# Fused attention and two feed-forward layers on one core: who adds the small constant to the row sums, and when the reciprocals stand in VectorE's queue

## The chip, the core and the metric

The kernel runs on one core of a Trainium2 chip. A core has TensorE (PE, matrix products into PSUM; its weight loads are listed as PEld), VectorE (DVE), ScalarE (ACT), GpSimd (POOL) and SyncE (SP, which issues most DMA transfers). Each engine works through its own queue in order; semaphores tie the queues together. The metric is the time of one execution in microseconds.

## The reference

Inputs are `q`, `k`, `v` (2 x 8 x 768 x 64), 16 cluster centroids per head, and the weights of two feed-forward layers. All is fp32.

```
q_assign, k_assign = argmax over the 16 normalised centroids, per head and token
scores = where(q_assign == k_assign, q @ k.T / 8, -1e9)
attn   = exp(scores - rowmax)
attn   = attn / (sum(attn) + 1e-9)          # the constant that is moved
x      = (attn @ v), heads side by side     # 1536 x 512
x      = rational(x @ w_in) @ w_out         # first layer, 512 -> 2048 -> 512
out    = layernorm(h * softmax(h)) @ w2_out # second layer, h = x @ w2_in, 512 -> 1024 -> 512
```

## The kernel before

Attention runs as 96 units: 16 heads (head `n` is batch `n // 8`, head `n % 8`) of 6 units (`t` = 0 to 5), each of 128 query rows by 768 keys. Unit number `idx` is 6n + t. For a unit TensorE computes the scores, negated and masked, in two halves of 384 columns (`unit_scores`, L405 and L411); VectorE takes the row minimum of that (`unit_max`, L416; called the unit's maximum below); ScalarE takes the exponent into `p` and adds up each row into a column of `rs` (`unit_exp`, L426). Every two units VectorE transposes `p` in 32 x 32 blocks into `pt` (`turn_p`, L454), and TensorE multiplies that with `v` a head later (`pv_step`, L466). The scores live in two PSUM slots `s` that take turns, so the scores of a unit wait for the exponent of the unit two before.

`rs[key]` holds the row sums of the two heads 2 key and 2 key + 1. They are whole after the last unit of the odd head, and are used in the next even head, 2 key + 2, whose units are 12 key + 12 to 12 key + 17. In its unit 0 `pair_sums` (L490) has GpSimd add the constant 1e-9 (L494) and puts the reciprocal on VectorE behind the maximum of its unit 2 (`step(12 * key + 14, "dve", ...)`, L495). `sums_out` (L505) puts the rest two steps on: in front of the scores of unit 3 TensorE turns the 128 x 12 reciprocals (`turned`, L511), into the free columns of that unit's PSUM slot; behind unit 3's exponent ScalarE copies them out (`rt`, L516), and SyncE sends them to DRAM (`rd`, L518) and back, spread over 64 partitions each (`rb`, L521). GpSimd then scales the pair's output with it (`pair_fin`, L539 and L553). For the last pair (key 7) ScalarE adds the constant (L497) and no DRAM is used.

GpSimd also prepares the operands of each head one head ahead (`prep_head`: L358 three times, L372, L377). With it go the mask rows, which SyncE copies into the prepared tiles (L381, L382). Between these stand parts of the weight conversion of the first layer (L149, L152, L164 on ScalarE, L156 on VectorE, L157 and L165 on GpSimd).

The order of each engine's queue is set when the program is built, by a scheduler that follows the order of the code and these constraints: `step(u, e, f)` issues `f` in unit `u` right behind that unit's instruction on engine `e`; `tc.issue_after(x)` holds what is issued inside it behind `x`; `behind` does so for one instruction. Without such a bound the scheduler may place an instruction earlier or later in its queue.

Of the kernel before, what the change touches and what calls it, by code (L numbers as in the profile page):

```python
# [10 lines left out]
AF = mybir.ActivationFunctionType  # L11
ALU = mybir.AluOpType
# [18 lines left out]
def fused_kernel(ctx: ExitStack, tc: tile.TileContext, qT, kT, v, cent, w1, w2i, w2o, gln, coef, centT, cst, tri, out):  # L31
    nc = tc.nc
# [14 lines left out]
    def psum2(tag, name):  # L47
        return ps[tag].tile([128, 2, 512], F32, name=name, tag=tag, bufs=2)
# [38 lines left out]
    tiny = const.tile([128, 1], F32, name="tiny")  # L87
# [105 lines left out]
    last = {}  # L193

    def load_pairs(es, parts=1):
        for pp, i in es:
            b, p = divmod(pp, 4)
            t = asp.tile([128, S], F32, name=f"pr{pp}{i}", tag="pr", bufs=4)
            raw["p", pp, i] = t
        w = S // parts  # L200
        for c in range(parts):
            for pp, i in es:
                b, p = divmod(pp, 4)
                nc.sync.dma_start(
                    out=raw["p", pp, i][:, w * c:w * c + w],
                    in_=(qT, kT)[i][b, 2 * p:2 * p + 2].rearrange("j d t -> (j d) t")[:, w * c:w * c + w])

    def load_head(n):
        b, h = divmod(n, H)
        for i, src in enumerate((qT, kT)):  # L210
            t = qk.tile([128, S], F32, name=f"dup{n}{i}", tag=f"dup{i}", bufs=2)
            if n:
                nc.sync.dma_start(out=t[0:64], in_=src[b, h])
            nc.sync.dma_start(out=t[64:128], in_=src[b, h])
            raw["d", n, i] = t

    def load_v(n):

        b, h = divmod(n, H)
        t = vp.tile([128, S // 32, D], F32, name=f"v{n}", tag="v", bufs=2)  # L220
        for r in range(4):
            nc.sync.dma_start(out=t[32 * r:32 * r + 32], in_=v[b, h])
        vv[n] = t
# [68 lines left out]
    def by_token(k, t, o):  # L292
        M = 32 * len(sets[k])
        return nc.tensor.transpose(o, E[k][0:M, t * 128:(t + 1) * 128], ident[0:M, 0:M])
# [69 lines left out]
    def prep_head(n, er=None, es=None):  # L364
        er = er or nc.gpsimd
        es = es or nc.gpsimd
        b, h = divmod(n, H)
        i = n % NB
        a, c = raw.pop(("d", n, 0)), raw.pop(("d", n, 1))
        rnd(er, k1[i], c, sgn[:, 1:2])  # L370
        yield
        es.tensor_tensor(k2[i][0:64], c[0:64], k1[i][0:64].bitcast(F32), op=ALU.subtract)  # L372
        yield
        rnd(er, q1[i], a, sgn[:, 0:1])
        rnd(er, q2[i][0:64], a[0:64], -0.125)
        yield
        es.tensor_tensor(q1[i][64:128], a[64:128], q1[i][64:128].bitcast(F32), op=ALU.subtract)  # L377
        yield
        if n:
            assert masked[next(k for k, es in enumerate(sets) if (n // 2, 0) in es)] == S  # L380
            nc.sync.dma_start(out=k2[i][64:80].bitcast(F32), in_=mk.pop((n, 1)).bitcast(F32))  # L381
            last["mk"] = last["mk", n] = nc.sync.dma_start(out=q2[i][64:80].bitcast(F32), in_=mk.pop((n, 0)).bitcast(F32))  # L382
        yield
# [13 lines left out]
    def unit_scores(n, t):  # L397
        i = n % NB
        sp = psum2("s", f"s{n}_{t}")
        sl = slice(t * 128, (t + 1) * 128)  # L400
        before = None
        for f in pre.pop(n * NT + t, ()):
            before = f(sp) or before
        for a in range(2):
            r = nc.tensor.matmul(sp[:, a, 0:384], lhsT=q1[i][:, sl], rhs=k1[i][:, a * 384:(a + 1) * 384], start=True, stop=False)  # L405
            if a == 0:
                last["pe0"] = r
            if before:
                behind(r, before)
        for a in range(2):  # L410
            last["pe"] = nc.tensor.matmul(sp[:, a, 0:384], lhsT=q2[i][:, sl], rhs=k2[i][:, a * 384:(a + 1) * 384], start=False, stop=True)  # L411
        return sp
# [20 lines left out]
    def step(u, e, f):  # L433
        steps.setdefault((u, e), []).append(f)
# [55 lines left out]
    def pair_sums(key):  # L490

        r = rs.pop(key)
        if key < 7:
            nc.gpsimd.tensor_scalar(r, r, 1.0, 1e-9, op0=ALU.mult, op1=ALU.add)  # L494
            step(12 * key + 14, "dve", lambda: nc.vector.reciprocal(r, r))  # L495
            return r
        nc.scalar.activation(out=r, in_=r, func=AF.Identity, bias=tiny)  # L497
        nc.vector.reciprocal(r, r)

        rw = fin.tile([128, S], F32, name="rw", tag="rb", bufs=1)  # L500
        nc.vector.tensor_copy(rw.rearrange("p (t j d) -> p j t d", t=NT, j=2), r[:, :, :, None].to_broadcast([128, 2, NT, D]))
        rb = psum2("s", "rbp")
        rsd[key] = rb, rw

    def sums_out(key, r, u):  # L505

        w = []

        def turned(sp):
            w.append(sp)  # L510
            return nc.tensor.transpose(sp[0:12, 0, 384:512], r.rearrange("p j t -> p (j t)"), ident)  # L511

        def spread_out():
            sp = w[0]
            rt = sm.tile([12, 128], F32, name=f"rt{key}", tag="rt", bufs=2)
            nc.scalar.activation(out=rt, in_=sp[0:12, 0, 384:512], func=AF.Copy)  # L516
            d = dram.tile([2, S], F32, name=f"rd{key}", tag="rd")
            nc.sync.dma_start(out=d.rearrange("j (t p) -> (j t) p", p=128), in_=rt)  # L518
            rb = fin.tile([128, S], F32, name=f"rb{key}", tag="rb", bufs=1)
            for j in range(2):  # L520
                nc.sync.dma_start(out=rb[64 * j:64 * j + 64], in_=d[j:j + 1, :].to_broadcast([64, S]))  # L521
            rsd[key] = rb

        while u in pre:
            u += 1
        pre[u] = [turned]
        step(u, "act", spread_out)
# [32 lines left out]
    def spread(gen, n, i0, i1, plan=plan):  # L560
        for i in range(n):
            plan[min(96, i0 + (i1 - i0) * i // n)].append(gen)
# [70 lines left out]
    for a in range(2):  # L633
        tps.append(bank(f"a{a}", f"set0{a}")[:, 0:3 * M].rearrange("p (t m) -> p t m", t=3))
        for t in range(3):
            r = by_token(0, 3 * a + t, tps[a][:, t])
# [98 lines left out]
    for idx, (n, t) in enumerate(units):  # L735
        if idx == ACL:
            asg.close()
            wh["r"] = ctx.enter_context(tc.tile_pool(name="wh2", bufs=4, side="right"))
        if idx in PAIRS:
            with tc.issue_after(last["mk"].ins):  # L740
                load_pairs(sets[PAIRS[idx]])
        if t == 3 and 0 < n < B * H - 2:
            with tc.issue_after(last["mk", n].ins):
                load_head(n + 2)
        if t == 0:
            if n >= 1 and n + 1 < B * H:
                spread(prep_head(n + 1), 7, idx, idx + 6)
        if t == (4 if n + 1 < B * H else 3):
            with tc.issue_after(last["mk"].ins):
                load_v(n)  # L750
        sp = unit_scores(n, t)
        run_steps(idx, "pe")
        m = unit_max(n, t, sp)
        run_steps(idx, "dve")
        if n == B * H - 1 and t >= NT - 2:
            if t == NT - 2:
                for _ in turn_p(n, NT // 2 - 2):
                    pass
            else:
                end = turn_p(n, NT // 2 - 1)  # L760
                next(end)
        elif t % 2 and idx > 1:
            for _ in turn_p(*divmod(idx // 2 - 1, NT // 2)):
                pass
        if idx == 8:
            with tc.issue_after(last["act"].ins):
                nc.scalar.activation(out=ab, in_=coef_t[:, 4:6], func=AF.Abs)

        m_, i0, i1 = pv_part(n, t)
        if m_ >= 0:  # L770
            for i in range(i0, i1):
                pv_step(m_, i)
        unit_exp(n, t, sp, m)
        run_steps(idx, "act")
        if t == 0 and n and n % 2 == 0:
            sums_out(n // 2 - 1, pair_sums(n // 2 - 1), idx + 3)
        for i, f in zip(SET1, (set1_a, set1_b, set1_c)):
            if idx == i:
                f()
        if n >= 2 and t == 1:  # L780
            for i in range(2):
                with tc.issue_after(last["act"].ins):
                    pv_out(n - 2, i)
            if n % 2:

                fin_ = pair_fin(n // 2 - 1)
                for i in (2, 3, 4, 5):
                    plan[min(96, idx + i)].append(fin_)
        run_plan(idx)
        if idx == 1:  # L790
            set1_0()
            with tc.issue_after(last["act"].ins):
                nc.scalar.activation(out=trib, in_=tri_t, func=AF.Copy)
# [369 lines left out]
```

## Time and profile before

| | us |
|---|---|
| runs shown | 648.45, 650.13, 650.15 (median 650.13) |
| the profiled execution | 653.5 |
| its span, first to last instruction | 651.6 |
| TensorE busy in it | 606.2 (93%) |
| VectorE busy | 478.6 (73%) |
| ScalarE busy | 443.3 (68%) |
| GpSimd busy | 393.6 (60%) |

The mean granted clock of TensorE is 0.982 of full speed. Busy times say which engine has much to do, not what a given stretch waits for; for that the rows below are read. In a row of a timeline the first number is the start in us from the first instruction of the span, the second the duration; the engine, the line of the kernel, the operation and its output and inputs follow, with the count of merged instructions, and in brackets how long the engine had been idle and which instruction ended that. A busy share of TensorE counts matrix products whose ends are modelled.

### The profile page before, as it was taken

The numbers are of one execution on the slowest core, as the hardware profiler recorded it, in microseconds if no ns is written. First come the engines' busy times: TensorE is split into PE (matmuls) and PEld (weight loads), VectorE is DVE, ScalarE is ACT, GpSimd is POOL, SyncE is SP. The second block draws the span as 40 slices with busy tenths as digits, with TensorE's granted clock in tenths as the row PEclk, the third lists the DMA queues.
The fourth block names the chain that finished last, engine by engine and source line by source line (L and its number), as shares of the span: only waits on it lengthen the run. The fifth ranks groups of instructions, "written<-read, shape, count | busy, mean of one in ns | idle before, by whom it ended". The sixth has DMA issues, their size and how long they took to land.

```text
span 651.6 us, 13967 instructions
## 1 busy us (share of the span) xinstructions
PE 606.2 (93%) x5601; PEld 480.0 (74%) x5601; DVE 478.6 (73%) x633; ACT 443.3 (68%) x804; POOL 393.6 (60%) x345
## 2 busy tenths in 40 slices
PE   7788888788976899999999999999999999999998
PEld 6466666566654688788888888886888888888887
DVE  3688789778968779887979878779798645344350
ACT  3567578657858678989988879789796334444251
POOL 5955588848979557998889988777976000000000
PEclk9799999989979899999999999999999999999999
DMA  8967968776765241221213323223000000000001
GB/s 207 226 169 189 246 160 238 188 183 174 203 160 122 74 165 65 98 96 66 97 65 99 97 65 97 65 65 89 10 1 1 1 18 16 33 17 17 32 16 49
DMA packets 22584, 64.79 MB, mean 99 GB/s; under 512 B 4548, under 2 KB 5784, under 8 KB 22520
## 3 DMA queue, kind: packets, MB, share of 16 engines
q1 hardware_dynamic: 22088, 63.73, 35.4%
q8 instruction: 44, 0.72, 0.5%
q10 hardware_dynamic: 432, 0.17, 0.1%
q14 instruction: 20, 0.16, 0.1%
HBM read 59.23 MB, written 3.19 MB: 96 GB/s over the span
## 4 chain that ended last, share of the span: by engine, by line
PE 54%; DVE 4%; ACT 4%; POOL 3%; issue 1%; POOLq 0%; DVEq 0%; ACTq 0%
PE y L912 16%; PE h L805 14%; PE hh L1000 10%; PE o L1051 10%; PE lt L1033 2%; PE pv L466 1%; POOL gl L895 1%; POOL q L876 1%; DVE q L887 1%; ACT y L874 1%; DVE vw L160 1%; DVE xhl L718 1%; POOL q L875 1%; ACT t L873 1%; DVE h L888 1%
## 5 line engine op out<-in xcount | busy, mean ns | idle before, releaser
L426 ACT ACTIVATE p<-s,m 128x768 f32<-128x768 f32 x96 | 86.1, 899 | 69.5 <-DVE m L416 69.1
L416 DVE TENSOR_REDUCE m<-s 128x1 f32<-128x768 f32 x96 | 88.9, 944 | 29.0 <-PE s L411 29.0
L805 PE MATMUL h<-xhl,w1h 128*128 128x512 f32 x336 | 106.5, 393 | 0.1
L466 PE MATMUL pv<-pt,v 32*64 32x192 f32 x3072 | 84.6, 339 | 4.8 <-ACT w L484 3.6
L454 DVE STREAM_TRANSPOSE pt<-p 128x1536 f32<-128x1536 f32 (+1 forms) x49 | 84.9, 1733 | 0.2 <-ACT p L426 0.2
L895 POOL TENSOR_TENSOR gl<-y,gh 128x512 fp32r<-128x512 f32 x48 | 71.3, 1488 | 16.7 <-ACT gh L894 16.5
L466 PEld LDWEIGHTS pv<-pt,v 32*64 32x64 f32 x3072 | 60.0, 134 | 23.2 <-issue 14.6
L805 PEld LDWEIGHTS h<-xhl,w1h 128*128 128x128 f32 x336 | 62.8, 188 | 14.9 <-DVE y L889 0.5
L405 PE MATMUL s<-k,q 128*128 128x384 f32 x192 | 59.6, 393 | 11.0 <-ACT p L426 10.1
L912 PE MATMUL y<-gl,w1h 128*128 128x512 f32 x168 | 66.1, 393 | 1.3 <-POOL gl L895 1.3
L876 POOL TENSOR_TENSOR q<-q,t 128x512 f32<-128x512 f32 x48 | 64.4, 1342 | 2.9
L912 PE MATMUL y<-gh,w1l 128*128 128x512 f32 x168 | 65.8, 392 | 0.0
L805 PE MATMUL h<-xhl,w1l 128*128 128x512 f32 x168 | 65.6, 392 | 0.0
L912 PE MATMUL y<-gh,w1h 128*128 128x512 f32 x168 | 61.7, 392 | 0.0
L875 POOL TENSOR_SCALAR q<-t,ab 128x512 f32<-128x512 f32 x48 | 42.3, 880 | 21.9 <-ACT t L873 16.2
L405 PEld LDWEIGHTS s<-k,q 128*128 128x128 f32 x192 | 31.0, 197 | 32.1 <-ACT p L426 18.0
L411 PE MATMUL s<-k,q 128*128 128x384 f32 x192 | 51.4, 351 | 1.7 <-POOL k L631 1.7
L1000 PE MATMUL hh<-vh,xhl 128*128 128x512 f32 x160 | 51.0, 395 | 0.0
L877 DVE TENSOR_TENSOR y<-y,h 128x512 f32<-128x512 f32 x48 | 32.8, 684 | 24.3 <-ACT y L874 24.0
L887 DVE SCALAR_TENSOR_TENSOR q<-q,h 128x512 f32<-128x512 f32 x47 | 32.0, 682 | 11.5 <-ACT h L885 11.0
L912 PEld LDWEIGHTS y<-gl,w1h 128*128 128x128 f32 x168 | 31.5, 188 | 9.6 <-POOL gl L895 2.7
L411 PEld LDWEIGHTS s<-k,q 128*128 128x128 f32 x192 | 36.5, 197 | 2.0 <-POOL k L631 2.0
(190 smaller groups left out, 1408.4 us busy)
## 6 DMA issues: line engine op xcount, KB each, us to landing
raww<-in_w SPq DMA_DIRECT2D x32, 512.0 KB, 3.7
v<-in_v SPq DMA_DIRECT2D x64, 192.0 KB, 5.9
dup<-in_qT SPq DMA_DIRECT2D x31, 192.0 KB, 5.8
dup<-in_kT SPq DMA_DIRECT2D x31, 192.0 KB, 5.1
rawv<-in_w2i SPq DMA_DIRECT2D x8, 512.0 KB, 3.6
rawv<-in_w2o SPq DMA_DIRECT2D x8, 512.0 KB, 3.6
out<-ob SPq DMA_DIRECT2D x11, 256.0 KB, 2.0
pr<-in_qT SPq DMA_DIRECT2D x7, 384.0 KB, 5.4
```

Source lines behind the costliest of these rows:

```text
L405: r = nc.tensor.matmul(sp[:, a, 0:384], lhsT=q1[i][:, sl], rhs=k1[i][:, a * 384:(a + 1) * 384], start=True, stop=False)
L411: last["pe"] = nc.tensor.matmul(sp[:, a, 0:384], lhsT=q2[i][:, sl], rhs=k2[i][:, a * 384:(a + 1) * 384], start=False, stop=True)
L416: last["dve"] = nc.vector.tensor_reduce(m, sp[:, :, 0:384], axis=AX.XY, op=ALU.min)
L426: last["act"] = nc.scalar.activation(out=P[n, t // 2][:, t % 2], in_=sp[:, :, 0:384], func=AF.Exp, scale=-1.0, bias=m, accum_out=rs[key][: ...
L454: r = nc.vector.transpose(PT[n][:, 2 * i + m * a:2 * i + m * a + m].rearrange("p t k -> p (t k)"), p[:, m * a:m * a + m].rearrange("p t a ...
L466: last["pv"] = nc.tensor.matmul(pv[n][64 * c:64 * c + 64, r, 0:192].rearrange("p (t q) -> p t q", t=NT), lhsT=vv[n][sl, j], rhs=PT[n][sl, ...
L805: r = nc.tensor.matmul(hp, lhsT=w[:, kt * 128:(kt + 1) * 128], rhs=x[:, kt], start=(i == 0), stop=(i == 11))
L876: nc.gpsimd.tensor_tensor(q, q, t, op=ALU.mult)
L895: nc.gpsimd.tensor_tensor(gl, y, gh.bitcast(F32), op=ALU.subtract)
L912: nc.tensor.matmul(o, lhsT=w[:, c], rhs=g, start=(first and i == 0), stop=(last and i == 2))
L1000: last["th"] = nc.tensor.matmul(hp[:, a], lhsT=y[:, kt], rhs=w[:, 512 * a:512 * a + 512], start=(kt == 0 and e == 0), stop=(kt == 3 and e ...
L1051: r = nc.tensor.matmul(op[:, 0:m], lhsT=l[:, kt], rhs=w, start=(n == 0), stop=(n == 23))
```

## The change

The constant is added by ScalarE for all pairs, by one ACTIVATE with function Identity and the constant as bias, issued behind the exponent of unit 0 of the even head. The reciprocal of pairs 0 to 6 is put behind the maximum of unit 1 of that head, where it stood behind that of unit 2. The transpose on TensorE stays in front of unit 3.

```diff
     def pair_sums(key):
 
         r = rs.pop(key)
+        nc.scalar.activation(out=r, in_=r, func=AF.Identity, bias=tiny)
         if key < 7:
-            nc.gpsimd.tensor_scalar(r, r, 1.0, 1e-9, op0=ALU.mult, op1=ALU.add)
-            step(12 * key + 14, "dve", lambda: nc.vector.reciprocal(r, r))
+            step(12 * key + 13, "dve", lambda: nc.vector.reciprocal(r, r))
             return r
-        nc.scalar.activation(out=r, in_=r, func=AF.Identity, bias=tiny)
         nc.vector.reciprocal(r, r)
...
         if t == 0 and n and n % 2 == 0:
-            sums_out(n // 2 - 1, pair_sums(n // 2 - 1), idx + 3)
+            with tc.issue_after(last["act"].ins):
+                sums_out(n // 2 - 1, pair_sums(n // 2 - 1), idx + 3)
```

The order that comes of it is shown for head 14 (pair 6). On VectorE, `m14_0` to `m14_3` are the maxima of units 0 to 3, `pt13` the transposed exponents of head 13, `rs6` the row sums of heads 12 and 13, and `w1f4` a weight in conversion. Before:

```order
L416 TENSOR_REDUCE m14_0_2971<-s14_0_2966 128x1
L416 TENSOR_REDUCE m14_1_2984<-s14_1_2979 128x1
L454 STREAM_TRANSPOSE pt13_2862<-p13_4_2919 128x1536
L416 TENSOR_REDUCE m14_2_3031<-s14_2_3026 128x1
L495 RECIPROCAL rs6_2589<-rs6_2589 128x12
L156 TENSOR_SCALAR w1f4_286<-w1f4_286 128x512
L416 TENSOR_REDUCE m14_3_3045<-s14_3_3039 128x1
```

VectorE at the same place now:

```order
L416 TENSOR_REDUCE m14_0_2971<-s14_0_2966 128x1
L416 TENSOR_REDUCE m14_1_2984<-s14_1_2979 128x1
L454 STREAM_TRANSPOSE pt13_2862<-p13_4_2919 128x1536
L495 RECIPROCAL rs6_2589<-rs6_2589 128x12
L416 TENSOR_REDUCE m14_2_3032<-s14_2_3027 128x1
L156 TENSOR_SCALAR w1f4_286<-w1f4_286 128x512
L416 TENSOR_REDUCE m14_3_3045<-s14_3_3039 128x1
```

The reciprocal has moved ahead of the maximum of unit 2, and stands behind the transpose. In heads 4 to 12 it is the same; in head 2 it stands ahead of the transpose as well.

On GpSimd, in the same head, `k11`, `q11`, `q21` and `k21` are the operands of head 15. Before:

```order
L358 TENSOR_SCALAR q21_170<-dup150_2849 64x768
L372 TENSOR_TENSOR k21_172<-dup151_2852,k11_171 64x768
L377 TENSOR_TENSOR q11_169<-dup150_2849,q11_169 64x768
L494 TENSOR_SCALAR rs6_2589<-rs6_2589 128x12
L157 TENSOR_TENSOR w1f4_286<-w1f4_286,raww141_2847 128x512
```

The addition stood behind the whole preparation of head 15 and is gone from this queue; the rest is in the old order. On ScalarE it appears behind the exponent of unit 0 of head 14 (`p14_0`, which the exponents of units 0 and 1 share; `u6` and `w6` are the product with `v` of head 12 being copied out):

```order
L426 ACTIVATE p14_0_2974,rs7_2973<-s14_0_2966,m14_0_2971 128x768
L493 ACTIVATE rs6_2589<-rs6_2589,tiny_94 128x12
L426 ACTIVATE p14_0_2974,rs7_2973<-s14_1_2979,m14_1_2984 128x768
L484 ACTIVATE u6_3021<-pv12_2864 64x4x6x32
L484 ACTIVATE w6_3022<-pv12_2864 64x4x6x32
```

Nothing else has moved on ScalarE, and SyncE's queue is as it was.

## Rows read from the trace of the kernel before

**Rows 1.** Summary of waits: engine, line, releaser; total us, times, longest us.

```profile
DVE m L416 <- PE s L411: 29.0, 40, 2.4
PE s L511 <- DVE rs L495: 18.4, 7, 4.9
DVE rs L495 <- POOL rs L494: 8.0, 3, 3.2
```

**Rows 2.** Table by stretch: heads 4, 8, 10, 12, 13, 14, first scores to first scores.

```profile
core 0: us, PE busy (x) PEld busy (x) DVE busy (x) ACT busy (x) POOL busy (x), PEclk, DMA share, GB/s
69.19:82.53 13.34, 11.58 (x254) 8.43 (x250) 10.27 (x11) 8.01 (x18) 6.46 (x7) 1.00 0.95 207
120.89:138.10 17.21, 13.79 (x254) 10.07 (x250) 10.64 (x12) 9.20 (x20) 10.50 (x10) 0.80 0.96 229
152.72:164.33 11.61, 9.96 (x225) 7.48 (x217) 10.74 (x12) 9.11 (x19) 8.51 (x8) 1.00 0.66 159
175.87:192.64 16.77, 11.94 (x226) 8.81 (x218) 10.98 (x12) 9.74 (x20) 13.07 (x13) 0.80 0.79 192
192.64:204.13 11.49, 10.04 (x225) 7.47 (x217) 11.34 (x11) 9.63 (x19) 10.82 (x10) 1.00 0.49 120
204.13:220.55 16.42, 11.49 (x226) 8.55 (x218) 10.98 (x12) 9.75 (x20) 12.28 (x11) 0.90 0.26 69
```

**Rows 3.** Timeline of TensorE, units 3 and 4 of heads 6, 8, 12, 14.

```profile
102.97 0.59 PE L405 MATMUL s<-k,q 128*128 128x384 f32 x2
...
105.00 0.62 PE L405 MATMUL s<-k,q 128*128 128x384 f32 x2
...
129.01 0.37 PE L511 MATMUL s<-cst,rs 128*12 128x128 f32 x1 [3.11 <-DVE rs L495]
...
184.83 0.37 PE L511 MATMUL s<-cst,rs 128*12 128x128 f32 x1 [4.75 <-DVE rs L495]
...
213.21 0.37 PE L511 MATMUL s<-cst,rs 128*12 128x128 f32 x1 [4.86 <-DVE rs L495]
213.23 0.99 PE L405 MATMUL s<-k,q 128*128 128x384 f32 x2
...
216.75 0.62 PE L405 MATMUL s<-k,q 128*128 128x384 f32 x2
```

**Rows 4.** Timeline of GpSimd in head 14.

```profile
210.71 1.80 POOL L377 TENSOR_TENSOR q<-dup,q 64x768 fp32r<-64x768 f32 x1
212.60 0.20 POOL L494 TENSOR_SCALAR rs<-rs 128x12 f32<-128x12 f32 x1
```

**Rows 5.** Timeline of VectorE in heads 6 and 14.

```profile
101.75 0.92 DVE L416 TENSOR_REDUCE m<-s 128x1 f32<-128x768 f32 x1
102.59 0.21 DVE L495 RECIPROCAL rs<-rs 128x12 f32<-128x12 f32 x1
...
103.95 0.96 DVE L416 TENSOR_REDUCE m<-s 128x1 f32<-128x768 f32 x1 [0.86 <-PE s L411]
...
207.02 1.76 DVE L454 STREAM_TRANSPOSE pt<-p 128x1536 f32<-128x1536 f32 x1
...
212.83 0.23 DVE L495 RECIPROCAL rs<-rs 128x12 f32<-128x12 f32 x1 [3.21 <-POOL rs L494]
...
214.90 0.96 DVE L416 TENSOR_REDUCE m<-s 128x1 f32<-128x768 f32 x1 [1.56 <-PE s L411]
```

**Rows 6.** Timeline of ScalarE: unit 0 of head 14; the addition for the last pair.

```profile
206.32 0.90 ACT L426 ACTIVATE p<-s,m 128x768 f32<-128x768 f32 x1 [0.36 <-DVE m L416]
207.12 0.19 ACT L426 ACTIVATION_READ_ACCUMULATOR p<-s,m 128x1 f32 x1
...
233.37 0.31 ACT L497 ACTIVATE rs<-rs,tiny 128x12 f32<-128x12 f32 x1
233.58 0.79 ACT L484 ACTIVATE u<-pv 64x768 f32<-64x768 f32 x1
```

**Rows 7.** Timeline of SyncE's queue in head 13 (spread sums, mask rows of head 14).

```profile
193.22 1.10 SPq L521 DMA_DIRECT2D rb<-rd  x2
...
195.01 0.58 SPq L382 DMA_DIRECT2D q<-oh  x1
```

**Rows 8.** DMA issues by line: count, KB each, median us from issue to landing.

```profile
q<-oh SPq DMA_DIRECT2D x15, 48.0 KB, 4.2
```

## The prediction

> **What bounds the kernel now.** I read the summary of waits first [rows 1], then the heads one by one in a table by stretch [rows 2], then each engine's timeline around the seven places where a reciprocal of row sums is taken. The program is 16 heads of attention, one after the other, and then the two feed-forward layers; the change touches heads alone, so the question is what a head is waiting for.
>
> The reader is to see in [rows 1] that TensorE stood still 18.4 us over exactly 7 occurrences, each time before the small transpose of the reciprocals (L511), and each time until VectorE had taken the reciprocal (L495). In three of the seven VectorE itself waited for GpSimd's addition (L494), 8.0 us together. [rows 3] has three of TensorE's seven waits: 3.11 us in head 8, 4.75 in head 12, 4.86 in head 14. The other four, in heads 2, 4, 6 and 10, share 18.4 - 12.72 = 5.7 us, 1.4 each.
>
> What makes GpSimd late is shown for head 14 in [rows 4]: the addition is a 0.20 us instruction that starts at 212.60, directly behind the last step of preparing head 15 (210.71 + 1.80 = 212.51). It waits for nothing but its place in the queue; the row sums of heads 12 and 13 were complete before head 14's first exponent at 206.32 [rows 6]. VectorE stops at its reciprocal from 209.6 to 212.83 [rows 5], and since TensorE's transpose stands ahead of the scores of unit 3, the maximum of unit 3 comes at 214.90. [rows 2] has the price in whole heads: 16.77 and 16.42 us for heads 12 and 14 against 11.61 for head 10, which has the same instructions but a GpSimd that was in time, and 17.21 for head 8 against 13.34 for head 4, its like (both also carry the similarities of a later set).
>
> The price is more than the idle time. In [rows 2] the granted clock of heads 8, 12 and 14 is 0.80, 0.80 and 0.90, so part of each ran at the lower level of 1.2 GHz; heads 4, 10 and 13, in which TensorE had no such gap, have 1.00, which is 2.4 GHz. [rows 3] shows it in the work: from the scores of unit 3 to those of unit 4 head 6 needs 105.00 - 102.97 = 2.03 us, head 14 behind its gap 216.75 - 213.23 = 3.52, so 1.49 more.
> The Trainium skill (TensorE: Matmul & The Clock Gate, HAM oscillation) says that the array's clock falls to half after TensorE has stood idle and that the work after the gap starts cold; the trace agrees, with 3.52 us against 2.03. By that page the slow stretch would go with the gap; without it only the idle 12.7 us would.
>
> **The change part by part.** *GpSimd's addition goes.* Seven instructions of 0.20 us, 1.4 us of queue; by itself worth nothing, since GpSimd is not what ends a head (0 to 1.4).
>
> *ScalarE gets it, behind the first exponent of the even head.* The one case in the trace is the addition for the last pair, L497: 0.31 us, the next instruction 0.21 us after it [rows 6]. So seven times 0.21 of queue and 0.31 until the result. In head 14 the exponent of unit 0 starts at 206.32; with its 0.90, the 0.19 of reading out the sum and 0.31 the addition would be done at about 207.7. The exponent of unit 1 moves back by 0.21 (1.5 us over seven heads, if nothing covered it). The cover is VectorE's transpose of 1.76 us from 207.02 to 208.78 [rows 5]: the reciprocal now stands behind it and ahead of the maximum of unit 2, so it finds its operand ready with 1.06 us to spare. In head 2 the order puts it ahead of the transpose; there I allow 0.2, the length of the reciprocal. If the cover were gone, each place would lose what ScalarE is late.
>
> *VectorE's reciprocals come one unit sooner.* Same number, same 0.23 us. In front of unit 2's maximum it delays that by 0.2, and no longer delays the transposed sums.
>
> *The three late places.* Head 14 step by step: the reciprocal can start at 208.78; from its start to TensorE's transpose it takes 213.21 - 212.83 = 0.38 [rows 3, 5], so TensorE goes on at 209.16 rather than 213.21: 4.05 us. With the slow 1.49 us that is 5.5. By whole heads it is 16.42 - 11.61 = 4.81 plus what head 10 itself gains (0.8, next part): 5.6. The two agree, and I take the heads: 5.6 for head 14; 16.77 - 11.61 + 0.8 = 5.96 for head 12; 17.21 - 13.34 + 0.8 = 4.7 for head 8. Sum 16.2. From below this is bounded by GpSimd's 8.0 us alone, from above by the idle 12.7 + 3 x 1.49 = 17.2.
>
> *The four other places.* Head 6 shows them [rows 5]: the maximum of unit 2 starts at 101.75 and holds the reciprocal up by its 0.84 us (next start 102.59); after it VectorE waits 0.86 us for the scores of unit 3. With the reciprocal ahead of that maximum the scores come about 0.8 earlier and VectorE can use it. 4 x 0.8 = 3.2, between 0 and the 5.7 of TensorE's waits.
>
> *What is late next.* Together 19.4 us, from which I take three things. VectorE is busy 10.98 us in heads 12 and 14 [rows 2], and the forecast lengths, 16.77 - 5.96 and 16.42 - 5.6, are both 10.8: 0.3 off for the two. The mask rows of the next head come through SyncE's queue behind the row sums' way through DRAM [rows 7]: at the start of head 13 SyncE issues the spread of the sums at 193.22 and the last mask rows of head 14 at 195.01, landing 4.2 us later [rows 8] at 199.2. Head 14 starts at 204.13 today; 5.96 earlier is 198.2. That chain begins with the exponent of unit 3, which moves too, but SyncE has loads in front that do not: 0.5 off. And in heads 4 and 8 the DMA engines are already busy 0.95 and 0.96 of the time [rows 2]; head 8's 16.5 us of transfers do not fit into 12.5, so loads have to move into neighbours (head 10 has 0.66): 0.6 off. That leaves **18.0 us**.
>
> The profiled execution took 653.5 us (span 651.6): 653.5 - 18.0 = 635.5. It was 3.4 us above the median of the three runs, 650.13; the saving belongs to both alike, so I forecast 650.1 - 18.0 = **632.1 us**. The saving passes to the end because everything behind the heads is released by their last unit.
>
> **The rivals.**
> *Given back to the next limit.* GpSimd is busy 13.07 + 10.82 us in heads 12 and 13 [rows 2], 23.9 us, and the forecast wants these two heads in 28.3 - 6.0 = 22.3. It prepares head 15 by 212.5, 8.0 us ahead of need (220.55), and the two savings take 11.6 from that need, so GpSimd must come 3.5 us earlier by closing its idle 3.7 + 0.7: it fits with 0.9 to spare. If it does not, heads 12 and 13 end at 23.9, a saving of 4.4. If also the transfers of head 8 stay where they are, it saves 17.2 - 16.5 = 0.7 and heads 2, 4 and 6 nothing. 0.7 + 4.4 + 5.6 + 0.8 = 11.5 us, 638.6; with less of each, 8 to 15, that is 635 to 642. For it: the thin margins. Against: head 13 and head 10 already run at 11.5 us with the same loads per head.
> *More than forecast.* Nothing is late next and the four short waits go whole: 17.2 + 5.7 = 22.9, 627.2. Against: VectorE is busy 10.74 of head 10's 11.61, so a head has less than a microsecond left to lose.
> *No change.* The reciprocal's wait would have to be hidden already, or its place taken by one just as long. Against: heads of equal work differ by 5 us just where GpSimd is late. 650.
> *Slower.* The reciprocal now waits for ScalarE with the maximum of unit 2, its exponent and the next scores queued behind it. With a margin of 1.06 us, a ScalarE that reaches the addition d us later than in the trace costs 7 x (d - 1.06); this eats the 18.0 from d = 3.6 on, and at d = 5 the kernel takes 650.1 + 27.6 - 18.0 = 659.7. For it: the addition's 0.21 us and the weight conversions stand in the same queue. Against: ahead of the exponent of unit 0 ScalarE waits 0.36 us for VectorE [rows 6], so it is not late at all.
> The same page of the Trainium skill (A second HAM failure mode) warns that many short idles can also make the clock swing; no head with waits of 1.4 us shows that here (1.00 in heads 4 and 10).
>
> **How the numbers follow.** Forecast 0.68, with 15 to 20.5 us saved, 629.6 to 635.1. Given back 0.18, more 0.07, no change 0.04, slower 0.03. The range that leaves out some two in ten takes in half of the giving back and of the excess: 628.5 to 639.5. About 0.3%, 2 us, is what can be told from no change here: faster 0.93, same 0.04, slower 0.03.
>
> **What would show it.** Right: no wait of VectorE's reciprocals for any engine, TensorE's waits before the transpose under 6 us in all; heads 12 and 14 between 10.8 and 11.6 us, head 8 between 12 and 13, the granted clock 1.00 in all three; the first feed-forward product of TensorE some 18 us earlier. Wrong in part: TensorE waiting for the next head's prepared operands or mask rows at the start of heads 9, 13, 14 or 15, or heads 8 and 12 stretched with the DMA share near 1. Wrong altogether: reciprocals waiting for ScalarE, or heads shorter and the feed-forward layers longer by the same amount.

## The result, and the profile after

The changed kernel takes 641.72 us, median of six runs (639.90 to 643.57), against 650.14 of the kernel before beside it. The ratio is 0.9858, with a 95% interval of 0.9811 to 0.9906: 1.4% faster, where 2.8% was forecast (632.1 us). The time lies above the range given. The profiled execution took 641.27 us with a span of 639.5; against the 651.6 of before that is 12.1 us, but the profiled execution of before lay 3.4 us above its median, so 8 to 9 us is the size to explain against 18.0. Where in the program those 3.4 us lie no run shows. In the two profiles 1.0 of the 12.1 us lies ahead of the first scores of head 1 (29.20 and 28.20), where nothing was changed and the order of the queues is the same; the other 11.1 lie in heads 1 to 15, and what follows the first product of the feed-forward layers (232.59 and 220.47) takes 419.0 us in both.

The summary of waits of the changed kernel answers to [rows 1] (the reciprocal is now L495, TensorE's transpose L510, the product with `v` still L466):

```profile
PEld pv L466 <- DMA v<-in_v: 4.7, 8, 1.0
...
PE s L510 <- DVE rs L495: 2.5, 4, 0.7
...
PE pv L466 <- DMA v<-in_v: 2.3, 6, 0.7
```

What the change says it does has happened. No reciprocal waits for another engine any more, and TensorE's waits ahead of the small transpose fell from 18.4 us to 2.5. New are the two rows with `v<-in_v`: TensorE waits for the load of `v`, 4.7 us in its weight loads and 2.3 us in its products. These overlap, so they are not to be added. The summary of before has no such row at all.

The table by heads (columns as in [rows 2]; heads 4, 8, 10, 12 and 14) tells where:

```profile
66.99:80.48 13.49, 12.46 (x254) 8.82 (x250) 10.14 (x11) 8.05 (x19) 6.43 (x6) 1.00 1.01 214
117.96:133.65 15.69, 14.08 (x253) 9.66 (x249) 11.48 (x12) 9.41 (x21) 11.88 (x11) 0.89 0.90 215
148.31:159.09 10.78, 10.04 (x226) 7.49 (x218) 10.77 (x12) 9.34 (x20) 8.35 (x8) 1.00 0.76 179
170.56:186.16 15.60, 14.29 (x225) 9.88 (x218) 12.13 (x12) 9.94 (x21) 14.53 (x14) 0.78 0.80 205
196.91:208.38 11.47, 10.23 (x226) 7.54 (x218) 11.47 (x12) 9.71 (x21) 11.16 (x10) 1.00 0.33 79
```

Head 14 went from 16.42 to 11.47 us with the granted clock at 1.00. Head 8 went only from 17.21 to 15.69 and head 12 from 16.77 to 15.60; both still have stretches at the lower clock (mean 0.89 and 0.78: with two levels, 1.00 and 0.50, that is 3.5 and 6.9 us at the lower one). Head 4 did not get shorter (13.34 to 13.49), with the DMA engines busy all the time.

TensorE's timeline in heads 8, 12 and 14 of the changed kernel, beside [rows 3]:

```profile
122.80 0.27 PE L510 MATMUL s<-cst,rs 128*12 128x128 f32 x1
...
123.27 0.51 PE L411 MATMUL s<-k,q 128*128 128x384 f32 x2
124.18 0.51 PE L466 MATMUL pv<-pt,v 32*64 32x192 f32 x2 [0.41 <-DMA v<-in_v]
124.86 0.53 PE L466 MATMUL pv<-pt,v 32*64 32x192 f32 x2 [0.17 <-DMA v<-in_v]
126.06 2.78 PE L466 MATMUL pv<-pt,v 32*64 32x192 f32 x44 [0.67 <-DMA v<-in_v]
126.64 1.59 PEld L466 LDWEIGHTS pv<-pt,v 32*64 32x64 f32 x42 [0.39 <-DMA v<-in_v]
...
176.41 1.18 PE L466 MATMUL pv<-pt,v 32*64 32x192 f32 x4
178.00 2.72 PE L466 MATMUL pv<-pt,v 32*64 32x192 f32 x44 [0.42 <-DMA v<-in_v]
...
201.82 0.27 PE L510 MATMUL s<-cst,rs 128*12 128x128 f32 x1 [0.41 <-DVE rs L495]
...
203.03 1.24 PE L466 MATMUL pv<-pt,v 32*64 32x192 f32 x48 [0.23 <-ACT w L484]
```

In head 14 the transpose, the scores of unit 3 and the 48 pieces of the product run on without a stop for `v`. In heads 8 and 12 the product of that same unit starts, stops for one of the four loads of `v` after the other (the last stop shows in the weight loads, PEld, alone), and its last 44 pieces then take 2.78 and 2.72 us where 48 take 1.24 in head 14: the idle time, and the lower clock behind it, have moved from the transpose to the product right behind it.

Why `v` comes then is in SyncE's queue. In the kernel before, the loads of the `v` of heads 7 and 11, which heads 8 and 12 multiply in unit 3, stand there so:

```profile
121.39 1.76 SPq L222 DMA_DIRECT2D v<-in_v  x4
...
173.77 1.76 SPq L222 DMA_DIRECT2D v<-in_v  x4
```

For those of head 7 the view of DMA issues gives the median time to landing (last number, us):

```profile
v<-in_v SPq DMA_DIRECT2D x4, 192.0 KB, 8.0
```

And TensorE's timeline has the two products that use them:

```profile
130.60 2.58 PE L466 MATMUL pv<-pt,v 32*64 32x192 f32 x48
...
186.41 2.22 PE L466 MATMUL pv<-pt,v 32*64 32x192 f32 x48
```

SyncE's queue at the same place of the changed kernel, and the `v` of head 11:

```profile
107.66 0.30 SPq L517 DMA_DIRECT2D rd<-rt  x1
111.82 1.10 SPq L520 DMA_DIRECT2D rb<-rd  x2
...
114.28 0.54 SPq L213 DMA_DIRECT2D dup<-in_kT  x1
...
117.15 0.54 SPq L132 DMA_DIRECT2D raww<-in_w  x1
117.79 1.76 SPq L222 DMA_DIRECT2D v<-in_v  x4
...
169.96 1.76 SPq L222 DMA_DIRECT2D v<-in_v  x4
```

The median time to landing for head 7 there:

```profile
v<-in_v SPq DMA_DIRECT2D x4, 192.0 KB, 7.4
```

In head 8 `v` was in time before only because the late transpose had pushed the product back: the last of the four loads landed at 130.9, the product started at 130.60, 9.7 us into the head. Now the product could start at about 124, 6 us into the head, and the last load lands only at 126.6, at the last stop in the rows above. In head 12 there was room before: `v` was whole at 182.1, 4.3 us ahead of the product. That room is gone from both sides. The product comes 4.7 us sooner within the head (5.8 us behind its first scores, 10.5 before), and `v`, issued 3.8 us sooner for a head that starts 5.3 us sooner, is whole 1.7 us later within it (7.9 us in, 6.2 before): the heads have become shorter, SyncE's queue has not kept up. Ahead of the loads of head 7 in the queue stand the row sums' way through DRAM (the spread of the sums, behind the write of 107.66, is not issued before 111.82), then 4 x 192 KB of `q` and `k` for head 10 and 512 KB of weights. The chain of waits over heads 4 to 14 goes through the `v` of heads 3, 7 and 11 (7.68, 7.34 and 7.11 us) and through that way through DRAM (4.14).

### The profile page after: what moved, and what is told of

The parts are those of the page before. It is cut to its first block, busy times and chain, and to the rows that moved or that the text cites. A ratio compares the mean times of both kernels' runs of the same rounds, so it can differ in the third digit from the quotient of the medians.

```text
span 639.5 us, 13958 instructions
## 1 busy us (share of the span) xinstructions
PE 607.1 (95%) x5601; PEld 478.6 (75%) x5601; DVE 480.1 (75%) x633; ACT 444.3 (69%) x811; POOL 392.6 (61%) x338
## 4 chain that ended last, share of the span: by engine, by line
PE 62%; DVE 14%; ACT 8%; DMA 6%; POOL 4%; issue 4%; SPq 2%; ACTq 0%; POOLq 0%; DVEq 0%
PE y L912 16%; PE h L805 15%; PE hh L1000 10%; PE o L1051 10%; DVE m L416 5%; DVE pt L454 4%; PE pv L466 4%; DMA v<-in_v 3%; ACT p L426 3%; PE s L405 2%; PE lt L1033 2%; PE s L411 2%; POOL gl L895 1%; DMA pr<-in_kT 1%; POOL q L876 1%
## 5 line engine op out<-in xcount | busy, mean ns | idle before, releaser
L466 PE MATMUL pv<-pt,v 32*64 32x192 f32 x3072 | 88.3, 337 | 7.5 <-ACT w L484 4.7
L466 PEld LDWEIGHTS pv<-pt,v 32*64 32x64 f32 x3072 | 61.1, 133 | 28.6 <-issue 13.4
L895 POOL TENSOR_TENSOR gl<-y,gh 128x512 fp32r<-128x512 f32 x48 | 71.3, 1489 | 16.7 <-ACT gh L894 16.5
L405 PE MATMUL s<-k,q 128*128 128x384 f32 x192 | 58.4, 386 | 11.3 <-ACT p L426 10.6
L405 PEld LDWEIGHTS s<-k,q 128*128 128x128 f32 x192 | 29.7, 191 | 33.1 <-ACT p L426 18.8
L411 PE MATMUL s<-k,q 128*128 128x384 f32 x192 | 49.9, 342 | 2.0 <-POOL k L630 2.0
L894 ACT ACTIVATE gh<-y 128x512 fp32r<-128x512 f32 x48 | 29.8, 628 | 11.6 <-DVE y L889 11.5
```

Of the source, the lines that this page charges most:

```text
L466: last["pv"] = nc.tensor.matmul(pv[n][64 * c:64 * c + 64, r, 0:192].rearrange("p (t q) -> p t q", t=NT), lhsT=vv[n][sl, j], rhs=PT[n][sl, ...
L895: nc.gpsimd.tensor_tensor(gl, y, gh.bitcast(F32), op=ALU.subtract)
```

## The experiments

Ratios are to the kernel before, timed beside each run; its median was 650.1 to 653.3 us, so runs are compared by ratio. The line numbers are those of the changed kernel unless said otherwise.

**The two halves apart.** ScalarE's addition alone, with the reciprocal left behind the maximum of unit 2:

```diff
-            step(12 * key + 13, "dve", lambda: nc.vector.reciprocal(r, r))
+            step(12 * key + 14, "dve", lambda: nc.vector.reciprocal(r, r))
```

> The changed kernel with the reciprocals back behind the maximum of unit 2: only the engine of the addition is changed against before. Theory (what mattered is GpSimd's queue): the reciprocals no longer wait for another engine, the three long idles of TensorE go, heads 2, 6 and 10 keep their short one of about 1.4 us; 642 to 646. Rival (the place of the reciprocal is what gave the time): above 647.

Measured: 644.30 us, ratio 0.9866 (0.9820 to 0.9911), not to be told from the whole change. Its waits, and heads 8 and 12:

```profile
PE s L510 <- DVE rs L495: 9.5, 7, 1.6
```

```profile
124.43:137.13 12.70, 11.11 (x253) 8.24 (x249) 10.90 (x12) 9.41 (x21) 9.36 (x9) 1.00 0.85 206
176.36:187.98 11.62, 9.98 (x226) 7.49 (x218) 11.53 (x12) 9.83 (x21) 11.47 (x10) 1.00 0.52 124
```

So the same time comes about in another way. The two heads are short, at full clock, and no wait of TensorE for `v` is listed in the whole run: the product comes about 1 us later within the head than in the changed kernel, and `v` is whole 6.3 and 5.1 us into it, where it takes 8.6 and 7.9 there. The time is lost in heads 1, 4, 6 and 10 instead (14.48, 15.25, 13.15 and 13.24 us, against 12.91, 13.34, 11.61 and 11.61 before). In head 6 the clock falls behind a wait of 1.56 us for the reciprocal (mean 0.87); in heads 4 and 10 TensorE also stands 1.33 and 1.39 us in a product for nothing that the profile shows. Why these stops and the loss in head 1 came in that execution stays open.

And the kernel before with only the reciprocal one unit sooner, behind GpSimd's addition:

```diff
-            step(12 * key + 14, "dve", lambda: nc.vector.reciprocal(r, r))
+            step(12 * key + 13, "dve", lambda: nc.vector.reciprocal(r, r))
```

> The kernel before with the reciprocals behind the maximum of unit 1, GpSimd still adding: only their place is changed. Theory: VectorE now waits for GpSimd's addition at all seven places, with the transpose and the maximum of unit 2 queued behind, so this is slower than before: 3 to 6 us of wait in each even head where 8.0 us in all stood, 655 to 670. Rival (the place of the reciprocal gave the time): 641 to 646.

Measured: 655.04 us, ratio 1.0064 (1.0037 to 1.0092).

```profile
DVE rs L495 <- POOL rs L494: 22.3, 6, 5.8
...
PE s L511 <- DVE rs L495: 11.8, 3, 4.9
```

So GpSimd's queue was the cause of the three late places, as forecast: without it no reciprocal waits for another engine and heads 8 and 12 are 4.5 and 5.2 us shorter, and with it an earlier reciprocal only waits longer (22.3 us where it was 8.0), at six places instead of three, with the maximum of unit 2 behind it.

**Are the bytes of `v` the new limit?** The changed kernel with a quarter of `v`: from head 2 on each of the four loads fills 8 of its 32 partitions, in a tile kept from two heads before, and the products use what stands there. The stale rows are left out of the load alone; every instruction of the engines stays.

```diff
-        t = vp.tile([128, S // 32, D], F32, name=f"v{n}", tag="v", bufs=2)
+        t = vp.tile([128, S // 32, D], F32, name=f"v{n}", tag="v", bufs=2) if n < 2 else vv[n - 2]
+        m = 32 if n < 2 else 8
...
-            nc.sync.dma_start(out=t[32 * r:32 * r + 32], in_=v[b, h])
+            nc.sync.dma_start(out=t[32 * r:32 * r + m], in_=v[b, h, 0:m])
```

> The changed kernel with a quarter of v's bytes from head 2 on: four loads as before, at the same place in SyncE's queue, of 8 partitions and not 32; the other rows keep the v of heads 0 and 1, so the attention output is left wrong from head 2 on. Theory A and rival B both expect v to land soon enough: the waits for v go, 632 to 636. Between them: if the landing of v falls from 7 us to 3 or less, it was the transfer, not the place in the queue, that was late. Rival C (GpSimd next): 638 to 642 with waits for its operands.

Measured: 633.66 us, ratio 0.9716 (0.9684 to 0.9749). No wait for `v` is left, and heads 4, 8 and 12 are about what the forecast wanted, at full clock:

```profile
66.53:78.35 11.82, 11.29 (x253) 8.49 (x250) 10.15 (x11) 8.07 (x19) 6.22 (x6) 1.00 0.55 135
117.57:129.39 11.82, 11.11 (x253) 8.31 (x249) 10.85 (x12) 9.21 (x21) 9.41 (x9) 1.00 0.59 142
166.38:177.70 11.32, 10.15 (x225) 7.51 (x218) 11.32 (x12) 9.69 (x21) 11.17 (x10) 1.00 0.39 98
```

The control is the same edit on the kernel before.

> The control to the run with a quarter of v, on the kernel before: from head 2 on each of the four loads of v brings 8 of its 32 partitions only, so that the product uses stale rows for the rest. Theory A: before the change GpSimd's late addition hides the late landing of v, and a quarter of v gains at most 2 us, 648 to 652 us. Rival B (the bytes of v cost the same in both kernels, so that the late addition hid nothing): the same 8 us as behind the change, 641 to 644 us.

Measured: 650.24 us, ratio 0.9958 (0.9934 to 0.9981). Three quarters of the bytes of `v` are worth 0.4% before the change and 1.4% behind it (0.9858 to 0.9716), and the wait of before stands there still (one line lower in this kernel):

```profile
PE s L512 <- DVE rs L496: 15.3, 6, 4.9
```

The late addition had hidden most of the late `v`; it had not hidden all of it. Read the other way, between these two kernels, in neither of which a wait for `v` is listed, the change is worth 0.9958 to 0.9716, 2.4% or some 16 us: close to the 18.0 forecast.

**Bytes or their order?** The same bytes in another order. First `v` at unit 2 of its head, with `q` and `k` for the later heads and the weights held behind it, and each weight asked for two units later (the last hunk):

```diff
-        if t == (4 if n + 1 < B * H else 3):
+        if t == 4 and n == 0:
             with tc.issue_after(last["mk"].ins):
                 load_v(n)
+        if t == 2 and n:
+            with tc.issue_after(last["pe"].ins):
+                load_v(n)
...
-            with tc.issue_after(last["mk", n].ins):
+            with tc.issue_after(last["v"].ins):
                 load_head(n + 2)
...
-        with tc.issue_after(last["mk", 4].ins) if nm in ("w100", "w101") else ExitStack():
+        with tc.issue_after(last["v"].ins):
             nc.sync.dma_start(out=raws[nm], in_=src)
...
-            for i in (-4, 0, 1, 3):
+            for i in (-2, 0, 1, 3):
```

> The changed kernel, but in heads 1 to 15 the four loads of v are issued two units sooner and stand on SyncE ahead of the next head's operand loads and of the raw weights, not behind them. Theory A (the gain in heads 4, 8 and 12 was handed to the load of v, which TensorE's product of units 3 waits for, 4.7 us in eight waits and a clock drop behind them): those waits go, heads 8 and 12 fall from 15.7 and 15.6 to about 12, head 4 from 13.5 to 12.5, and the time from 641.7 to about 634. Rival B (the DMA engines have no room left, whatever comes first): v lands sooner, but operands or weights then land later, some other wait for DMA of the same size appears, 640 to 643. Rival C (GpSimd's preparation of the next head is the next limit): v no longer waits, TensorE waits for GpSimd's operands at the start of heads 9 and 13, 638 to 642.

Measured: 654.65 us, ratio 1.0046 (1.0020 to 1.0071), above what any of the three theories gave. No wait for `v`, but three others:

```profile
ACT w1f L149 <- DMA raww<-in_w: 20.8, 7, 4.4
...
POOL k L358 <- DMA dup<-in_kT: 14.7, 7, 4.0
...
DVE rs L495 <- ACT rs L493: 7.8, 4, 3.0
```

This edit put off too much: the weights came late for ScalarE at seven places, and the addition stands in the same queue as their conversion. It is the one run in which the rival of a late ScalarE took place at more than one place. `v` can go only ahead of loads that are early themselves, and the next runs move less.

Only the weights behind `v`, nothing else moved:

```diff
-        with tc.issue_after(last["mk", 4].ins) if nm in ("w100", "w101") else ExitStack():
+        with tc.issue_after(last["v"].ins):
             nc.sync.dma_start(out=raws[nm], in_=src)
...
-            nc.sync.dma_start(out=t[32 * r:32 * r + 32], in_=v[b, h])
+            last["v"] = nc.sync.dma_start(out=t[32 * r:32 * r + 32], in_=v[b, h])
```

> Starts from the changed kernel (641.7 us). Only the loads of the first layer's weights are put behind the load of v in SyncE's queue; the loads of q and k for later heads stay ahead of it, so in heads 3, 7 and 11 v comes down one load of 256 KB, some 2 us, sooner. Theory A (v, landing late for the product in unit 3 of heads 4, 8 and 12, is the new limit): the waits for v shrink by about 2 us at each place, the kernel takes 636 to 640 us. Rival B (the DMA engines are simply full, whatever is last is late): the weights come late instead, ScalarE waits for them, 641 to 646 us. Rival C (v is not what sets the time): waits change places, time within 2 us of 641.7.

Measured: 633.97 us, ratio 0.9733 (0.9701 to 0.9766). (A load of weights is 512 KB in the profile, not the 256 of the expectation.) That is below the 636 to 640 of theory A: two lines, and the time is within 2 us of the prediction's forecast, with every byte loaded. Its waits, and heads 4, 8, 12, 13:

```profile
PE s L510 <- DVE rs L495: 2.8, 4, 0.7
...
PEld pv L466 <- DMA v<-in_v: 2.0, 3, 0.7
...
PE pv L466 <- DMA v<-in_v: 1.0, 3, 0.4
```

```profile
64.49:76.39 11.90, 11.51 (x254) 8.49 (x250) 10.16 (x11) 8.07 (x19) 6.22 (x6) 1.00 0.91 223
113.93:128.17 14.24, 12.72 (x253) 8.78 (x249) 11.99 (x12) 9.42 (x21) 12.38 (x11) 1.00 0.88 235
...
165.14:176.45 11.31, 10.17 (x225) 7.51 (x218) 11.31 (x12) 9.69 (x21) 11.16 (x10) 1.00 0.66 172
176.45:187.83 11.38, 10.10 (x216) 7.38 (x216) 11.22 (x11) 9.75 (x19) 10.28 (x8) 1.00 0.78 194
```

Heads 4 and 12 have their gain back, 1.6 and 4.3 us shorter than after the change alone, and the granted clock is 1.00 in head 8 too, though it still waits for `v`. There `v` is no sooner: it is whole 8.7 us into the head, 8.6 in the changed kernel, as the row sums' way through DRAM held SyncE's queue 6.5 us in this execution (from the write to the issue of the spread), where it was 4.2. So the 1.4 us that head 8 gained are, as far as the rows show, the clock's, which stayed up over stops of 0.22 to 0.39 us; in heads 4 and 12, where `v` is 4.6 and 4.4 us in, the gain is the order of the loads.

Then the loads of `q` and `k` behind `v` as well, with `v` at its old place behind the mask rows:

```diff
-            with tc.issue_after(last["mk", n].ins):
+            with tc.issue_after(last["v"].ins):
                 load_head(n + 2)
```

> Starts from the changed kernel. The loads of q and k for the head two on, and those of the weights, are both held behind the load of v that is being issued; v itself stays in its old place behind the mask rows. In heads 3, 7 and 11 v comes down 1 to 1.5 MB, about 4 to 5 us, sooner, with the same bytes in all. Theory A (order in the queue, not bytes): no wait for v left at the product in heads 4, 8 and 12, heads 8 and 12 at 12 to 13 us, the kernel 633 to 637 us. Rival B (bytes: others are late by as much): waits for weights or for q and k in place of those for v, 641 to 648 us.

Measured: 635.55 us, ratio 0.9753 (0.9725 to 0.9780). No wait of TensorE for `v`, but head 8 is as long as before that edit:

```profile
118.14:132.36 14.22, 11.47 (x254) 8.28 (x250) 11.75 (x12) 9.11 (x21) 12.62 (x12) 1.00 1.01 236
```

There the DMA engines are busy throughout; the mask rows were late for TensorE by 1.50 us and the spread of the row sums for GpSimd by 4.5 in that stretch. Order alone does not empty it. Heads 1, 4 and 6 are longer than with the weights alone behind `v` (15.87, 13.09 and 12.22 us against 12.92, 11.90 and 10.80).

The same at one place only, `q` and `k` for head 10 behind the `v` of head 7, the rest as with the weights behind `v`:

```diff
-            with tc.issue_after(last["mk", n].ins):
+            with tc.issue_after((last["v"] if n == 8 else last["mk", n]).ins):
                 load_head(n + 2)
```

> The run with the weights behind v, and in head 7 alone also the loads of q and k for head 10 behind v. Only SyncE's queue changes, at one place. Theory A (the 3.0 us that TensorE still waits for v in head 8, and the half clock or idle behind them, go): head 8 at 12 to 13 us in place of 14.24, the kernel 0 to 2 us faster, 631.5 to 634 us. Rival B (q and k for head 10 then come late for GpSimd, or the mask rows behind them for head 9): 634 to 638 us.

Measured: 635.24 us, ratio 0.9730 (0.9685 to 0.9775), not to be told from the run without it. Head 8 does come down, and head 12, where nothing was edited, goes up by nearly as much, waiting for its own `v`:

```profile
114.21:126.83 12.62, 11.22 (x253) 8.32 (x250) 11.89 (x12) 9.13 (x21) 12.47 (x12) 1.00 0.86 219
163.63:176.32 12.69, 11.09 (x225) 7.86 (x217) 11.06 (x12) 9.95 (x21) 12.54 (x11) 1.00 0.82 213
```

And `v` and the mask rows ahead of the spread as well, so that only loads behind them wait for the row sums' way through DRAM (in odd heads; the edit's core, the weights and `q` and `k` being held behind `v` as well):

```diff
-            for j in range(2):
-                nc.sync.dma_start(out=rb[64 * j:64 * j + 64], in_=d[j:j + 1, :].to_broadcast([64, S]))
             rsd[key] = rb
+            def spread_in():
+                with tc.issue_after(last["v"].ins):
+                    for j in range(2):
+                        nc.sync.dma_start(out=rb[64 * j:64 * j + 64], in_=d[j:j + 1, :].to_broadcast([64, S]))
+            step(12 * key + 20, "act", spread_in)
...
-        if t == (4 if n + 1 < B * H else 3):
-            with tc.issue_after(last["mk"].ins):
+        if t == (2 if n % 2 and n > 1 else 4):
+            with tc.issue_after(last["pe" if t == 2 else "mk"].ins):
                 load_v(n)
```

> As the run before with v first, and in the odd heads v and the mask rows also go ahead of the spread of the row sums, whose wait for its way through DRAM (4 to 5 us at the head of SyncE's queue) then holds up only the loads behind it. Theory A: v and the mask rows land 4 us sooner still; since v was in time already this adds at most 2 us, 632 to 637 us. Rival B: the spread comes late for GpSimd's scaling of the output, or q and k behind it come late for GpSimd's preparation, and GpSimd's queue holds the next head up: 638 to 650 us.

Measured: 641.28 us, ratio 0.9845 (0.9806 to 0.9883). Rival B: the spread now comes late for GpSimd's scaling (L556 in this kernel), whose queue holds the preparation of the next head.

```profile
POOL xf L556 <- DMA rb<-rd: 20.8, 6, 4.5
```

**What the earlier reciprocal is worth once `v` is out of the way.** The run with the weights behind `v`, and the reciprocal behind the maximum of unit 2 again:

```diff
-            step(12 * key + 13, "dve", lambda: nc.vector.reciprocal(r, r))
+            step(12 * key + 14, "dve", lambda: nc.vector.reciprocal(r, r))
```

> The run with the weights behind v (634.0 us, 0.973 of before), but with the reciprocals behind the maximum of unit 2 again, as before the change; ScalarE keeps the addition. It tells what the earlier place is worth once v is not in the way. Theory A (the four short places of 0.8 us, and the three others by the like): 3 to 5 us slower, 636.5 to 639 us, with VectorE's maximum of unit 2 again ahead of the reciprocal and TensorE's waits for it at 8 us or more. Rival B (the scheduler's other work covers the later place): 633 to 635.5 us, no difference that can be told.

Measured: 637.55 us, ratio 0.9768 (0.9723 to 0.9812), against 633.97 and 0.9733 with the earlier place: 2.3 us by the ratios, 3.6 by the medians. The intervals touch, so the time alone does not settle it; the waits point the same way, 8.5 us ahead of the transpose against 2.8.

```profile
PE s L510 <- DVE rs L495: 8.5, 6, 1.6
```

## Why the prediction was wrong, step by step

*What bounds the kernel* was right: the reciprocals' wait for GpSimd's queue, and with it the clock. The two halves apart show it (0.9866 with ScalarE's addition alone, 1.0064 with the earlier reciprocal alone). Of the signs that it named, no reciprocal waits for an engine, the waits before the transpose are under 6 us, and head 14 is in its range; heads 8 and 12 and their clock are not.

*ScalarE gets it*: right. 0.29 us where 0.31 was taken, the next exponent 0.20 us behind its start, and the reciprocal runs as its queue comes to it. ScalarE and VectorE in head 14 after the change, which answer to [rows 5, 6]:

```profile
200.28 0.29 ACT L493 ACTIVATE rs<-rs,tiny 128x12 f32<-128x12 f32 x1
200.48 0.89 ACT L426 ACTIVATE p<-s,m 128x768 f32<-128x768 f32 x1
```

```profile
201.49 0.18 DVE L495 RECIPROCAL rs<-rs 128x12 f32<-128x12 f32 x1
201.59 0.89 DVE L416 TENSOR_REDUCE m<-s 128x1 f32<-128x768 f32 x1
202.41 1.35 DVE L156 TENSOR_SCALAR w1f<-w1f 128x512 uint32<-128x512 uint32 x1
```

The addition is done at 200.57 and is used at 201.49, 0.92 us to spare where 1.06 was worked out.

*The three late places*, 16.2 us: right in size for what goes, wrong in that it stays gone. Head 14 gave 4.95 of its 5.6, so the working by whole heads and by the lower clock holds there. Heads 8 and 12 gave 1.52 of 4.7 and 1.17 of 5.96, together 8.0 us too little. With a quarter of `v` they are 11.82 and 11.32 us long; the kernel before with a quarter of `v` has 15.56 and 16.31, so the change takes 3.7 and 5.0 us out of them once `v` is not late: most of the two terms was there to be had.

*The four other places*, 3.2 us: near in size. The waits ahead of the transpose did go, to 2.5 us over all seven places, and heads 2, 6 and 10 gave 1.20, 0.82 and 0.83 us. In head 4 the gain is lost (0.15 us longer), as it waits for `v` as heads 8 and 12 do. With the weights behind `v` the earlier place is worth 2.3 to 3.6 us over all seven places, near the term, though its time alone does not settle that.

*What is late next* is the step that failed. It named the mask rows, GpSimd and the share of the DMA engines, and took 0.6 us off for the transfers, as loads that have to move into neighbours. What it had at nothing is one load: the `v` of the head before, needed by the product right behind the very scores that were to come 3 to 5 us sooner. In place of the 0.6 us, it took 8.0 us of the saving in heads 8 and 12 and the whole of head 4's. The rows for it stood in the trace of before: for head 8 issued from 121.39 to 123.15, 8.0 us to landing, product at 130.60; for head 12 a room of 4.3 us, less than the 5.96 that the head was to lose. A product that comes 3.7 and 4.7 us sooner within these heads meets a `v` that comes no sooner than SyncE's queue lets it, and that queue stands still for the sums' way through DRAM a head earlier (107.66 to 111.82 in the changed kernel). The summary of waits of before could not show it, since `v` was in time for the late product. And here too the price is more than TensorE's idle time: in head 8 its products stand 1.25 us for `v` (0.41 + 0.17 + 0.67), and the last 44 pieces take 1.5 us more than 48 do in head 14, at the lower clock and with the last stop for `v` among them. One end is open: with ScalarE's addition alone heads 8 and 12 have their gain and `v` is in time, and yet that kernel is no faster, for losses in other heads that the rows explain only in part.

*The rival "given back to the next limit"*, at 635 to 642 us, is what came in time, and by one of its two halves. Its length of head 8 was near (15.69 us, where it put 16.5), though what held the head was one late load and not the sum of the transfers: with the same bytes in another order it took 12.62. Its GpSimd half did not come: heads 12 and 13 together take 22.69 us in the run with the weights behind `v`, against the 23.9 that it set as the floor for GpSimd and the 22.3 that the forecast wanted. The loss in head 12, which the rival would have laid to GpSimd, was `v` too. *Slower* by a late ScalarE did not come in this kernel.

That the two-line repair (0.9733) meets the forecast (632.1 / 650.1 = 0.9723) within its interval is in part luck: it also mends what `v` cost the kernel before (a quarter of `v` gave 0.4% there), and head 8 is still 14.24 us long where 12.5 was forecast. Of the two runs that took TensorE's wait for `v` out of head 8, one left the head as long, and the other gave 12.62 us there and lost nearly as much in head 12. How to have both heads short without fewer bytes stays open.

The version that beats both kernels is thus the changed one with the loads of the weights behind those of `v`: 633.97 us, 2.7% under the kernel before.

## What to carry to other kernels

When a wait is removed, look in the trace for what arrives just inside it: for each operand of the instructions behind the wait, set its landing (issue plus the time to landing) against the new start, operand by operand. A summary of waits lists only the one that ended last, so an operand that has a few microseconds of room, or none, does not show there: here the room was none in head 8 and 4.3 us in head 12, and the product was to move by more. The loads do not keep their distance either, when their queue has a wait of its own in it. And where the next limit is a load, the order in its queue is the first thing to try, moving only what is early enough: one kind of load put back gave 1.3% here, a second kind on top of it nothing more, and putting both behind a `v` issued two units sooner, with the weights asked for later, lost 1.9%.

## What the runs showed of the hardware

A short VectorE instruction is stretched beside GpSimd. L156 (128 x 512, TENSOR_SCALAR) takes 0.36 to 0.41 us where no GpSimd instruction overlaps it. Beside GpSimd's L377 it took 1.12 to 1.17 us in three places of the kernel before (heads 7, 11 and 13). The change has put it beside L372 in heads 8, 12 and 14 as well, where it takes 1.42, 1.75 and, at 202.41 in head 14 above, 1.35 us. GpSimd there:

```profile
201.65 1.82 POOL L372 TENSOR_TENSOR k<-dup,k 64x768 fp32r<-64x768 f32 x1
```

Each time L156 ends 0.3 us behind the end of the GpSimd instruction: in heads 8, 12 and 14 at 125.30 against 125.00, 177.80 against 177.52, 203.76 against 203.47. That looks like waiting and then running, not like running slowly. The Trainium skill (SBUF — State Buffer, SBUF: two separate sides) describes it so: the two engines share a pair of ports, and where VectorE's instruction takes that pair, the one that starts first holds it for a whole instruction while the other stands still. The trace agrees, with 0.3 us left after GpSimd's end. In heads 8 and 12 TensorE was waiting for `v` then, and no cost can be told. In head 14 it seems to be a side effect of the change that was not forecast: the maximum of unit 3 starts 0.9 us behind the end of its scores (202.80, 203.67), and from the transpose on the head takes 6.5 us where head 10, whose L156 takes 0.41, needs 5.9. No run moves L156 alone, so this is not shown.

Short stops of TensorE can bring the lower clock, and need not. In the changed kernel it fell behind stops of 0.41, 0.17 and 0.67 us in head 8 (mean 0.89) and of 0.69 and 0.42 us in head 12 (mean 0.78), but not behind 0.33 and 0.30 in head 4, nor behind 0.22, 0.37 and 0.39 in head 8 of the run with the weights behind `v` (1.00 in both). What tells these cases apart no run shows.
